# The attention's v loads are issued by ACT, at the end of each period

## The chip, the cores and the metric

The kernel runs on one core of a Trainium2 chip. A core has five engines, each with its own queue in program order: TensorE (PE; its weight loads are listed as PEld), VectorE (DVE), ScalarE (ACT), GpSimd (POOL) and SyncE (SP), which computes nothing and issues DMAs. Data moves between device memory and on-chip memory through 16 DMA engines. The metric is the device time of one execution in microseconds, given as the median of several runs; lower is better.

## What is computed

Two stages in 32-bit floats. First an attention in blocks of 64 positions, for 8 batches of 576 positions with 8 heads of 64:

```python
scores = scale * np.matmul(q_c, k_c.transpose(0, 1, 2, 4, 3))   # per block of 64
scores = scores - np.max(scores, axis=-1, keepdims=True)
attn = np.exp(scores)
attn = attn / (np.sum(attn, axis=-1, keepdims=True) + 1e-09)
out = np.matmul(attn, v_c)
```

Then a mixture of experts on the result x, with 4608 tokens of 512 and 8 experts of 512 x 1024 x 512. Each token goes to one expert:

```python
fresh_e = int(np.argmax(logits[b, s]))
if s == 0 or local_gate[b, s] < 0.5:
    e = fresh_e
else:
    e = prev_e if prev_e >= 0 else fresh_e
h = np.maximum(x[b, s] @ w1[e], 0.0)
out[b, s] = p[e] * (h @ w2[e])
```

## The kernel before

The attention works on 18 blocks of 256 tokens. For a block, `load_qk` (lines 115 to 130) brings q and k as `qt` and `kt`, `load_v` (132 to 141) brings v in four DMAs of 64 positions each. POOL regroups q and k by pairs of heads (`qr`, `kr`); PE transposes them (`tr`), ACT copies the results out (`qT`, `kT`, line 154). Then come the scores (`sc`, line 193), their row maxima and the subtraction on DVE (204, 207), the exponential on ACT (`pr`, 212), the transposes of `pr`, copied out by ACT (`pT`, 154), and the values: 32 matmuls for each half of the heads (`o`, line 242), which read v. DVE divides by the row sums and writes `xs` (lines 254 to 256). `xs` is transposed and copied out (`xT`), the router's logits are computed from it (`lg`, line 284), copied to `lT` (289), transposed back (293) and summed into `L` (299); line 302 stores `xs` with its logits to the device array `x_d`, from which the expert stage later gathers its tokens by index.

Buffers: v has two (`NV = 2`, line 112), used in turn; `qt` and `kt` three each; `xs` three; `pr` and `pT` two.

These steps are interleaved over blocks. The loop at line 754 plays 15 periods, i = 1 to 15; in each, the string `steady` says in which order the pieces are emitted:

```python
"steady": "lq s*8 s ra*2 h0 tp*8 va*4 s va h1 ra*2 tq*16 h2 va*4 va lv tx*8 s h3 pr*4 ",
```

Here `lq` loads q and k of block i+5, `s` are the scores of block i+1 (eight groups of matmuls, then the maxima, the subtraction, the exponential), `ra` the router of block i-3, `tp` the transposes of `pr` of block i, `va` the values of block i-1, `tq` the transposes of q and k of block i+2, `lv` the v load of block i+1, `tx` the transposes of `xs` of block i-2, `pr` the regrouping of block i+3, and `h0` to `h3` are places for pieces of the routing in late periods. After the played pieces, some periods append work on expert 0's weights: a load into `raw` (lines 764, 766), and in periods 4 to 11 a split of a piece of w1 into a high part, cast by ACT (`w1h`, line 96), and the rest, subtracted by DVE (`w1l`, line 97).

In the loop the order on PE, DVE, ACT and POOL is exactly the emitted one (`manual_schedule`); each engine runs its queue in that order and waits where a semaphore says so. SP's order is set by the planner. Before the loop, v of blocks 0 and 1 is loaded at line 479, outside of any order by hand; after it, the string `drain` orders the last blocks together with the first tiles of the expert stage, and `ld` in it is the v load of block 17. The expert stage then runs tiles of 128 tokens, with matmuls of lines 627 and 641.

All 72 v DMAs, like every other direct load and store, are issued by SP.

Of the kernel before, what the change touches and what calls it, by code (L numbers as in the profile page):

```python
# [56 lines left out]
    "t0": "VAVA",  # L57
    "t1": "AAAA",
    "t2": "AVAA",
    "steady": "lq s*8 s ra*2 h0 tp*8 va*4 s va h1 ra*2 tq*16 h2 va*4 va lv tx*8 s h3 pr*4 ",  # L60
    "hooks": [47, 47, 49, 49, 51, 52, 52, 52, 53, 53, 55, 56, 56, 57, 58, 60, 62, 62],
}

# [2 lines left out]
def tile_attention_then_moe(ctx: ExitStack, tc, q, k, v, wg, wl, w1, w2, out):  # L66
    nc = tc.nc
# [64 lines left out]
    def load_v(i):  # L132
        vt = vbuf[i % NV]
        for ch in range(4):
            t0 = 256 * i + 64 * ch
            b, s0 = t0 // S, t0 % S
            nc.sync.dma_start(
                vt[64 * (ch // 2):64 * (ch // 2) + 64, ch % 2, :, 0:D],
                v[b, :, s0:s0 + 64, :].rearrange("h s d -> s h d"),
            )  # L140
        return vt
# [164 lines left out]
    def ok(i):  # L306
        return 0 <= i < NS
# [125 lines left out]
    def a_pair(i, engs=(nc.gpsimd,) * 4):  # L433
        hd[i], fns = pair_heads(qk.pop(i), engs)
        return fns
# [13 lines left out]
    def a_tx(i, fine=False):  # L449
        xTs[i] = pa2.tile([P, 4, 256], F32, name="xT", bufs=1)  # L450
        return x_transposes(xss[i], xTs[i], fine)

    def a_ra(i, fine=False):
        return router(i, xTs.pop(i), xss.pop(i), fine)
# [19 lines left out]
    for i in range(3):  # L474
        qk[i] = load_qk(i, 2 if i == 0 else 1)
        if i == 0:
            nc.gpsimd.memset(wg9, 0.0)
        else:
            vts[i - 1] = load_v(i - 1)
    nc.sync.dma_start(wg9[:, :, 0:8], wg.rearrange("(c p) e -> p c e", p=P))  # L480
    nc.sync.dma_start(wg9[:, :, 8:9], wl.rearrange("(c p) e -> p c e", p=P))
    with tc.manual_schedule(engines=MAN):
        def load(store, fn, i):
            def go():
                store[i] = fn(i)
            return lambda: [go]
# [267 lines left out]
    for i in range(1, NS - 2):  # L754
        qs4 = dict(s=lambda: a_sa(i + 1), tp=lambda: a_tp(i), va=lambda: a_va(i - 1, True), tq=lambda: a_tq(i + 2))
        opt = dict(lq=load(qk, load_qk, i + 5) if ok(i + 5) else None,
                   lv=load(vts, load_v, i + 1) if ok(i + 1) else None,
                   pr=(lambda: a_pair(i + 3)) if ok(i + 3) else None, tx=(lambda: a_tx(i - 2)) if i >= 2 else None, ra=(lambda: a_ra(i - 3, True)) if i >= 3 else None)
        for h in range(4):
            opt[f"h{h}"] = (lambda h=h: [lambda: run(hooks[i, h])]) if (i, h) in hooks else None  # L760
        toks = [t for t in PAR["steady"].split() if opt.get(t.split("*")[0], 1) is not None]
        play(" ".join(toks), qs4 | {k: v for k, v in opt.items() if v is not None})
        if 1 <= i < 5:
            load_w1(0, i - 1)
        if i in (6, 8, 10, 12):
            load_w2(0, i // 2 - 3)
        if 4 <= i < 12:
            c, col = divmod(i - 4, 2)
            col = slice(512 * col, 512 * col + 512)
            split(w1h[c][:, col], w1l[c][:, col], raw1[c][:, col])  # L770
# [30 lines left out]
    def gather_full(t):  # L801
# [25 lines left out]
    ]  # L827
    queues = dict(
        s=lambda: sa, ld=load(vts, load_v, n), rt=lambda: sb, rk=sb_rank, of=lambda: offsets, oh=sb_onehots,
        sl=lambda: slots([pc, pc, pc], QB[1], QB[2], ((0, NT),), qs), ex=lambda: experts,  # L830
        g=lambda: [lambda t=t: gather_full(t) for t in (EARLY, EARLY + 1)],
# [148 lines left out]
```

## Time and profile before

| | us |
|---|---|
| median of three runs | 729.97 (729.54 to 731.80) |
| the profiled execution | 728.45 |
| its span, first to last instruction | 726.7 |
| PE busy over the span | 659.7 |
| ACT busy over the span | 270.7 |
| first and last start of a v load | 5.1 and 182.5 |

Times in the profile count from the start of the span. A row of the timeline gives the start, the duration, the engine, the line and the operation with what it writes and reads, a count where rows are merged, and in brackets how long the engine stood idle before it and what ended that. `SPq` is SP's queue: the duration of a DMA there is the time for which the issue held the queue, not the time of the transfer. In the windows view each engine has its busy time and its number of instructions, followed by PE's granted clock (1.00 is full speed), the mean busy share of the 16 DMA engines, and what they moved. DMA issues are not counted as busy time of an engine.

The page's list of DMA issues (operation, count, size of each, median time from issue to landing) has these of the attention:

```profile
x_d<-xs SPq DMA_DIRECT2D x18, 521.0 KB, 6.8
v<-in_v SPq DMA_DIRECT2D x72, 128.0 KB, 5.8
qt<-in_q SPq DMA_DIRECT2D x11, 512.0 KB, 6.5
kt<-in_k SPq DMA_DIRECT2D x11, 512.0 KB, 7.8
```

and the DMA queues (packets, megabytes, share of the 16 engines' span):

```profile
q1 hardware_dynamic: 96608, 75.70, 41.1%
q0 software_dynamic: 6160, 19.85, 8.3%
```

q1 is SP's queue, q0 that of POOL's indirect transfers.

### The profile page before, as it was taken

How to read it: one execution, taken by the hardware profiler on the slowest of the kernel's cores; microseconds unless marked ns; L12 is line 12 of the kernel's file. 1: busy time of each engine (PE TensorE's matmuls, PEld its weight loads, DVE VectorE, ACT ScalarE, POOL GpSimd, SP SyncE). 2: the span in 40 equal slices, each digit the busy share in tenths (PEclk: the TensorE clock that was granted, in tenths of full speed). 3: DMA queues.
4: the chain of work that ended last, by engine and by line, in shares of the span. 5: the costliest groups of instructions: out<-in, count | busy, mean ns of one | idle time of the engine just before them, and what ended most of it. 6: DMA issues, size and time to landing. Idle time of an engine off the chain costs nothing. (4 is left out here: it accounts for less than half of the span.)

```text
span 726.7 us, 17109 instructions
## 1 busy us (share of the span) xinstructions
PE 659.7 (91%) x5594; PEld 523.6 (72%) x5594; DVE 369.0 (51%) x860; ACT 270.7 (37%) x432; POOL 177.1 (24%) x222
## 2 busy tenths in 40 slices
PE   4786878878999999999999999999999999999981
PEld 4665666666677788777888887778877888777861
DVE  2564655788685585356232563472586323454310
ACT  3564655656422234441222443422454222432210
POOL 3321222234022233223121231331243212231100
PEclk9998999999999999999999999999999999999986
DMA  9999999968723144145111352441276211234100
GB/s 211 207 211 275 257 241 236 272 144 191 229 89 118 46 161 141 57 142 173 33 48 43 95 171 83 147 156 47 90 240 221 75 47 35 89 121 140 40 29 15
DMA packets 102928, 97.49 MB, mean 134 GB/s; under 512 B 42672, under 2 KB 79536, under 8 KB 102768
## 3 DMA queue, kind: packets, MB, share of 16 engines
q1 hardware_dynamic: 96608, 75.70, 41.1%
q0 software_dynamic: 6160, 19.85, 8.3%
q8 instruction: 78, 1.28, 0.8%
q14 instruction: 82, 0.67, 0.3%
HBM read 76.48 MB, written 19.56 MB: 132 GB/s over the span
## 5 line engine op out<-in xcount | busy, mean ns | idle before, releaser
L641 PE MATMUL y<-w2h,hp 128*128 128x512 f32 x608 | 204.7, 407 | 9.8 <-DVE hp L591 6.2
L627 PE MATMUL h<-w1h,xp 128*128 128x512 f32 x608 | 178.3, 403 | 0.0
L641 PEld LDWEIGHTS y<-w2h,hp 128*128 128x128 f32 x608 | 115.8, 191 | 38.9 <-DVE hp L591 8.9
L627 PEld LDWEIGHTS h<-w1h,xp 128*128 128x128 f32 x608 | 111.4, 189 | 23.9 <-ACTq L861 0.2
L641 PE MATMUL y<-w2l,hp 128*128 128x512 f32 x304 | 121.9, 401 | 0.0
L700 POOL DMA_INDIRECT out<-ysb,sidx x38 | 41.1, 1082 | 274.3 <-DVEq L861 197.0
L627 PE MATMUL h<-w1l,xp 128*128 128x512 f32 x304 | 95.9, 397 | 0.0
L590 ACT CAST hp<-tr 128x512 fp32r<-128x512 f32 x76 | 41.2, 589 | 107.7 <-PE tr L588 100.7
L591 DVE TENSOR_TENSOR xp<-tr,xp 128x512 fp32r<-128x512 f32 x39 | 27.0, 691 | 104.6 <-ACTq L861 66.9
L699 DVE TENSOR_SCALAR ysb<-y,ppr 128x512 f32<-128x512 f32 x35 | 26.2, 748 | 94.2 <-PE y L641 81.7
L627 PEld LDWEIGHTS h<-w1l,xp 128*128 128x128 f32 x304 | 57.0, 188 | 14.7 <-DVEq L861 0.7
L641 PEld LDWEIGHTS y<-w2l,hp 128*128 128x128 f32 x304 | 58.2, 191 | 12.4
L680 ACT ACTIVATE hsb<-h 128x1024 f32<-128x1024 f32 x35 | 36.0, 1027 | 67.0 <-PE h L627 64.3
L591 DVE TENSOR_TENSOR hp<-tr,hp 128x512 fp32r<-128x512 f32 x76 | 49.3, 686 | 13.8 <-ACT hp L590 12.1
L613 ACT ACTIVATE pex<-pex 128x8 f32<-128x8 f32 x38 | 7.9, 209 | 119.8 <-DVE pex L612 119.8
L97 DVE TENSOR_TENSOR w1l<-raw,w1h 128x1024 fp32r<-128x1024 f32 (+1 forms) x29 | 40.9, 1428 | 22.9 <-ACT w1h L96 22.7
L594 POOL DMA_INDIRECT xg<-x_d,gidx x36 | 36.6, 1017 | 41.0 <-issue 24.4
L156 POOL COPY qr<-qt 128x512 f32<-128x512 f32 x34 | 20.0, 617 | 101.1 <-issue 71.3
L242 PE MATMUL o<-v,pT 64*64 64x65 f32 x1152 | 29.0, 232 | 16.4 <-DVE xs L256 12.6
L588 PE MATMUL tr<-ident,hsb 128*128 128x128 f32 x304 | 40.2, 273 | 0.3 <-ACT hsb L680 0.3
L242 PEld LDWEIGHTS o<-v,pT 64*64 64x64 f32 x1152 | 22.6, 140 | 24.8 <-DVE xs L256 15.2
L97 DVE TENSOR_TENSOR w2l<-raw,w2h 128x1024 fp32r<-128x1024 f32 x21 | 39.9, 1953 | 0.9 <-issue 0.9
(173 smaller groups left out, 832.9 us busy)
## 6 DMA issues: line engine op xcount, KB each, us to landing
raw<-in_moe_w SPq DMA_DIRECT2D x72, 512.0 KB, 4.6
x_d<-xs SPq DMA_DIRECT2D x18, 521.0 KB, 6.8
v<-in_v SPq DMA_DIRECT2D x72, 128.0 KB, 5.8
qt<-in_q SPq DMA_DIRECT2D x11, 512.0 KB, 6.5
kt<-in_k SPq DMA_DIRECT2D x11, 512.0 KB, 7.8
qt<-in_q SPq DMA_DIRECT2D x6, 256.0 KB, 6.3
kt<-in_k SPq DMA_DIRECT2D x6, 256.0 KB, 6.2
qt<-in_q SPq DMA_DIRECT2D x4, 384.0 KB, 6.1
```

What stands on the lines that cost most here:

```text
L97: (lo_eng or nc.vector).tensor_tensor(lo, raw, hi.bitcast(F32), ALU.subtract)
L156: eng.tensor_copy(dst, src)
L242: nc.tensor.matmul(o[64 * cp:64 * cp + 64, cc, DV * h:DV * h + D + 1], pT[64 * cc:64 * cc + 64, 4 * j + h, 64 * cp:64 * cp + 64], vt[64 * ...
L588: nc.tensor.transpose(ps[:, n], src_of(n), ident)
L590: return [tr, lambda: nc.scalar.copy(hi, box["ps"]), lambda: V.tensor_tensor(lo, box["ps"], hi.bitcast(F32), ALU.subtract)]
L591: lambda: V.tensor_tensor(lo, box["ps"], hi.bitcast(F32), ALU.subtract)]
L594: nc.gpsimd.indirect_dma_start(out=dst, out_offset=None, in_=src, in_offset=bass.IndirectOffsetOnAxis(ap=gidx[t].bitcast(U32), axis=0))
L627: nc.tensor.matmul(hs[:, j], xs[a][:, c], W1[w][c][:, 512 * j:512 * j + 512], start=(c == 0 and n == 0), stop=(c == 3 and n == 2))
L641: nc.tensor.matmul(y, hx[f // 4][a][:, f % 4], W2[w][c][:, f % 2, :], start=(f == 0 and n == 0), stop=(f == 7 and n == 2))
L680: nc.scalar.activation(hsb, hs.rearrange("p j f -> p (j f)"), AF.Relu)
L699: either(mix, lambda: V.tensor_scalar(ysb, y, pr, None, ALU.mult), lambda: y_mixed(ysb, y, ym, pr))
L700: nc.gpsimd.indirect_dma_start(out=out, out_offset=bass.IndirectOffsetOnAxis(ap=sidx[t].bitcast(U32), axis=0), in_=ysb, in_offset=None, bo ...
```

## The change

The four DMAs of `load_v` are issued by ACT instead of SP, everywhere it is called: before the loop, in it and in the drain. In the loop the load's place in the emitted order moves from before the x transposes (`tx`) to behind them and behind the last `s`, which is the exponential. As ACT's order is the emitted one, its four issues stand there between the exponential and what the period appends.

```diff
-    "steady": "lq s*8 s ra*2 h0 tp*8 va*4 s va h1 ra*2 tq*16 h2 va*4 va lv tx*8 s h3 pr*4 ",
+    "steady": "lq s*8 s ra*2 h0 tp*8 va*4 s va h1 ra*2 tq*16 h2 va*4 va tx*8 s lv h3 pr*4 ",
...
         for ch in range(4):
             t0 = 256 * i + 64 * ch
             b, s0 = t0 // S, t0 % S
-            nc.sync.dma_start(
+            nc.scalar.dma_start(
                 vt[64 * (ch // 2):64 * (ch // 2) + 64, ch % 2, :, 0:D],
                 v[b, :, s0:s0 + 64, :].rearrange("h s d -> s h d"),
             )
```

The bytes, the buffers and the number of DMAs stay the same.

## The prediction

> **What bounds the kernel now.** Read first the page's head, then the busy time by stage (the windows view), because the change touches only the attention, which fills the first quarter of the span.
>
> ```profile
> span 726.7 us, 17109 instructions
> PE 659.7 (91%) x5594; PEld 523.6 (72%) x5594; DVE 369.0 (51%) x860; ACT 270.7 (37%) x432; POOL 177.1 (24%) x222
> ```
>
> ```profile
> core 0: us, PE busy (x) PEld busy (x) DVE busy (x) ACT busy (x) POOL busy (x), PEclk, DMA share, GB/s
> 60.00:70.00 10.00, 6.93 (x152) 5.84 (x152) 3.84 (x9) 3.47 (x6) 0.00 (x0) 0.66 1.13 267
> ...
> 160.00:170.00 10.00, 8.20 (x188) 6.45 (x188) 9.72 (x32) 5.36 (x9) 8.28 (x15) 1.00 0.49 107
> ...
> 0.70:146.00 145.30, 110.05 (x2272) 89.45 (x2272) 77.78 (x183) 78.09 (x133) 38.95 (x92) 0.94 1.13 241
> ...
> 113.24:124.97 11.73, 8.64 (x171) 6.90 (x170) 6.07 (x15) 6.11 (x11) 2.28 (x4) 0.89 1.06 252
> 124.97:133.39 8.42, 7.69 (x171) 6.29 (x170) 5.57 (x14) 5.62 (x10) 2.28 (x4) 0.95 1.20 246
> ```
>
> The last two rows are one period each of the steady loop, from one start of the scores to the next: 8.42 us when nothing stalls, 11.73 when something does. PE works about 8 us of each, so 8.42 is near its floor. Up to 146 us the DMA engines are full (a share of 1.13, since packets overlap). SP's own timeline shows what that does to the queue that issues all loads and stores (columns: start, duration, queue, line):
>
> ```profile
> 36.63 5.71 SPq L137 DMA_DIRECT2D v<-in_v  x4
> ...
> 45.25 4.92 SPq L137 DMA_DIRECT2D v<-in_v  x4
> ...
> 56.68 3.63 SPq L137 DMA_DIRECT2D v<-in_v  x4
> ...
> 103.75 0.57 SPq L302 DMA_DIRECT2D x_d<-xs  x1
> 104.42 4.24 SPq L137 DMA_DIRECT2D v<-in_v  x4
> 108.70 1.76 SPq L93 DMA_DIRECT2D raw<-in_moe_w  x1
> 110.55 1.32 SPq L125 DMA_DIRECT2D qt<-in_q  x1
> ...
> 152.18 2.92 SPq L137 DMA_DIRECT2D v<-in_v  x4
> ```
>
> Each begins within 0.1 us of the end of the one before: SP is held by the engines it feeds. At 152 us, with the DMA share near a half, the same four v loads still hold it 2.92 us. What does this cost the compute engines? The waits of DVE between 26.9 and 172.3 us, and one stall in the timeline:
>
> ```profile
> DVE xs L256 <- DMA x_d<-xs: 12.1, 6, 5.5
> ```
>
> ```profile
> 121.41 0.69 DVE L256 TENSOR_TENSOR xs<-o,rs 128x512 f32<-128x512 f32 x1 [2.14 <-DMA x_d<-xs]
> ```
>
> DVE may not overwrite an xs buffer until the store that read it has landed; that is the stall of the 11.73 period. PE pays twice for it (its own timeline):
>
> ```profile
> 111.59 0.70 PE L242 MATMUL o<-v,pT 64*64 64x65 f32 x32
> 112.22 1.09 PE L164 MATMUL tr<-ident,xs 128*128 128x128 f32 x8
> 113.24 1.16 PE L193 MATMUL sc<-kT,qT 64*64 64x64 f32 x64
> ...
> 122.16 0.99 PE L242 MATMUL o<-v,pT 64*64 64x65 f32 x32 [1.97 <-DVE xs L256]
> 123.08 1.97 PE L164 MATMUL tr<-ident,xs 128*128 128x128 f32 x8
> 124.97 1.52 PE L193 MATMUL sc<-kT,qT 64*64 64x64 f32 x64
> ...
> 161.15 0.70 PE L242 MATMUL o<-v,pT 64*64 64x65 f32 x32 [1.94 <-DVE xs L256]
> ```
>
> After 1.97 us of idleness the same three groups take 4.48 us in place of 2.95: 1.53 more at a lower granted clock (0.89 in that window, 0.66 in the worst). After 1.94 us at 161.15 the first group, 0.70 us, did not slow. So an idle stretch of about 2 us costs the slow clock in some cases, and I charge half of 1.53, 0.75.
>
> **The change part by part.** It removes four issues per period from SP, which has no compute behind it, and puts them on ACT, which has. The cost is worked out from ACT's order at a period's end, with DVE and PE beside it (timeline of all engines, the rows of a stall-free end; the issues will stand between the first and the second row):
>
> ```profile
> 93.76 1.07 ACT L212 ACTIVATE pr<-pr 128x1024 f32<-128x1024 f32 x1
> ...
> 94.71 0.62 ACT L96 CAST w1h<-raw 128x512 fp32r<-128x512 f32 x1
> ...
> 95.37 0.69 DVE L97 TENSOR_TENSOR w1l<-raw,w1h 128x512 fp32r<-128x512 f32 x1 [2.00 <-ACT w1h L96]
> 95.57 1.07 ACT L154 COPY pT<-tr 128x512 f32<-128x512 f32 x2 [0.24 <-PE tr L164]
> 95.90 0.70 PE L242 MATMUL o<-v,pT 64*64 64x65 f32 x32
> 95.98 1.28 DVE L204 TENSOR_REDUCE mx<-sc 128x8 f32<-128x512 f32 x2
> ...
> 97.18 0.41 DVE L289 COPY lT<-lg 128x256 f32<-128x256 f32 x1
> ...
> 97.65 0.44 PE L293 MATMUL lg<-ident,lT 128*128 128x128 f32 x2 [1.05 <-DVE lT L289]
> ```
>
> *How long ACT is held.* Call it L. The trace has no DMA issued by ACT; SP's durations for these very transfers are the nearest (all v issues, minimum, median and maximum):
>
> ```profile
> L137 SPq DMA_DIRECT2D v<-in_v x72: 595/765/2243, 5.1 to 182.5; - x72
> ```
>
> The bounds are 4 x 0.595 = 2.38 us and the 5.71 at 36.63; I take the median, 4 x 0.765 = 3.06 us. A wait for the buffer adds nothing: its last reader, the second group of values, runs ahead of the x transposes whose copies ACT has already made.
>
> *From when.* The cast starts 0.95 us after the exponential starts, 0.12 before that one's end, so ACT hands out work ahead of an end; how far, the trace does not show. I let the issues begin with the exponential's start. At the other end, after its end, each period costs 1.07 us more; the other way, one copy ahead, about 0.5 us less (an estimate: the two pT copies of the row at 95.57 take 1.07 together). The Trainium skill (PSUM — Partial Sum Buffer, Engine vs sequencer instructions) says the sequencer waits only for earlier instructions to be dispatched, which is the value I take; no run here shows it yet.
>
> *Periods with a weight split (eight, loop passes 4 to 11).* The cast slips from 0.95 after the exponential's start to L, 2.1 later. DVE stands in order behind it: w1l, the row maxima and the lT copy, and PE's logit transpose waits for lT already now. ACT's pT copy and PE's values slip as much. So PE loses 2.1, plus 0.75 for the clock, on a floor of 8.42: 11.3 us. The eight intervals behind these loads now run between two starts of the scores (PE's timeline):
>
> ```profile
> 34.15 1.16 PE L193 MATMUL sc<-kT,qT 64*64 64x64 f32 x64 [0.22 <-ACT kT L154]
> ...
> 66.04 1.93 PE L193 MATMUL sc<-kT,qT 64*64 64x64 f32 x64
> ...
> 143.41 1.16 PE L193 MATMUL sc<-kT,qT 64*64 64x64 f32 x64
> ```
>
> 143.41 - 66.04 = 77.4; eight times 11.3 is 90.4: **+13.0**. The removed store waits are in this already, as the floor is a stall-free period: with v gone from SP a store no longer queues behind the last period's v loads.
>
> *The three before (34.15 to 66.04, 31.9 us).* No split there; what slips is the pT copy, 1.81 after the exponential's start. The three v rows of that stretch, 5.71, 4.92 and 3.63, average 4.75; less 1.81 is 2.95. Three times (8.42 + 2.95 + 0.75) = 36.4: **+4.5**, although the long stall of 5.5 us goes.
>
> *The four after (from 143.41).* 2.92 - 1.81 = 1.1 each; DVE, busy 9.72 of 10 us at 160 to 170, sets the pace there, so I count half: **+2.2**, from 0 to 4.4.
>
> *Start and drain.* The first two loads are eight issues ahead of all else on ACT: 8 x 0.765 = 6.1 us against ACT's first work at
>
> ```profile
> 6.01 1.28 ACT L154 ACT_TABLE_LOAD   x1 [6.01 <-DMA qt<-in_q]
> ```
>
> and they share the engines with the first q and k. But SP reaches the third block of q and k earlier. **+1.5**, from -3 (q and k early) to +6. The drain's load holds ACT once while PE has other work: **+1**, from 0 to 2.9.
>
> Sum: 13.0 + 4.5 + 2.2 + 1.5 + 1 = +22.2. The profiled execution took 728.45; the median of the runs is 729.97, 1.5 higher. 728.45 + 22.2 + 1.5 = **752 us**. Nothing later is touched: the expert stage is released by the routing at the attention's end and shifts as a whole.
>
> **The rivals.**
>
> *Faster: the store waits go and ACT's hold is hidden.* Place: the boundary between periods. For it: DVE's 12.1 us of waits and the clock lost behind them stand in the trace, and ACT is busy only 5.6 of 8.42 us. With no hold at all the eight intervals give 77.4 - 67.4 = 10 and the three 31.9 - 25.3 = 6.6, so -16.6 is the bound; the full DMA engines keep about half of it: -9, **721 us**. It decides from L of about 2.5: there (no clock loss) the eight give +2.4, the three (8.42 + 0.7) x 3 = 27.4, -4.5, the rest some +2, in all nil. Four issues at the least duration seen, taken one copy ahead, pass that point. Against it: L has been that short only on an unloaded queue, and a period this short loads it.
>
> *No change: the transfers set the pace.* SP's queue is never empty until 146 us; if the engines' work alone makes a period 9.7 us, holds and stalls trade places: **730 us**, 728 to 732. The stall-free 8.42 periods speak against it.
> The Trainium skill (DMA: Bandwidth & Descriptors, Issuing engines are not separate DMA queues) says that all queues run on the same 16 engines and a second issuer saves only issue time; by it this change has no bandwidth to gain.
>
> *Much slower: the two queues hold each other up.* If an issue of ACT must wait while one of SP is being taken, L grows by SP's blocked issues. The weight row and the store row (1.76, 0.57) stand near the boundary, so about +2: L = 5.1, and the clock lost every time: 8 x (8.42 + 4.15 + 1.53) = 112.8, +35; the three 8.42 + 4.95 + 1.53 each, +13; with the rest some +54: **784 us**.
> The Trainium skill (Perfetto Trace Analysis, DMA Instruction — HWDGE (DVE, Sync)) describes one descriptor generator, locked by one sequencer at a time; that is this rival's rule, and with a single issuer before, the trace can neither bear it out nor refute it.
>
> **How the numbers follow.** Forecast, ACT's hold outweighs the stalls: 0.64 (735 to 768 by L from 2.7 to 3.6 and the start of the hold). Faster rival 0.18, no change 0.08, mutual hold 0.10. A measurement of this kernel can tell about 0.3% (2 us) from no change, so: faster 0.18, same 0.08, slower 0.74. The range drops about half of the fast rival and most of the slowest: 722 to 772.
>
> **What would show it.** Right: ACT's queue shows four v issues of 0.6 to 1 us behind each exponential; the cast and the pT copy start later after it by L; PE's values wait for ACT and its logit transpose for lT; DVE's waits for the x store vanish; stalled or not, the steady intervals are near 11 us; the windows there show a clock under 0.95 and a smaller DMA share. Wrong: ACT's issues under 0.5 us each, or intervals below 9.7; a clock of 1.00 would take 0.75 off each; if store waits remain, SP was not what delayed the stores; issues above 1.2 us speak for the mutual hold.

## The result, and the profile after

| | before | after |
|---|---|---|
| median, us | 730.62 (729.54 to 731.80) | 753.89 (750.96 to 754.24) |
| ratio, with its 95% interval | | 1.0326 (1.0298 to 1.0355) |
| span of the profiled execution | 726.7 | 749.2 |
| mean granted TensorE clock | 0.974 | 0.972 |

The change makes the kernel 3.3% slower. The forecast was 752. (The median of before is now of four runs, the 729.97 given ahead was of three.) First the head of the page of after, and its rows by stage (PE, PEld, DVE, ACT, POOL busy, then the clock, the DMA share and GB/s); the last three rows are the stretches that the prediction priced:

```profile
span 749.2 us, 17059 instructions
...
PE 659.5 (88%) x5594; PEld 524.9 (70%) x5594; DVE 369.6 (49%) x860; ACT 271.8 (36%) x432; POOL 177.6 (24%) x222
```

```profile
0.70:146.00 145.30, 97.79 (x1968) 81.56 (x1968) 62.83 (x144) 68.38 (x115) 34.55 (x84) 0.91 1.05 220
75.05:163.59 88.54, 64.79 (x1366) 52.60 (x1365) 49.45 (x122) 48.10 (x82) 18.53 (x32) 0.94 0.97 197
163.59:193.22 29.63, 23.69 (x534) 18.69 (x532) 23.46 (x79) 15.80 (x28) 11.66 (x20) 1.00 0.42 115
193.22:231.50 38.28, 33.13 (x424) 24.17 (x423) 23.25 (x64) 16.57 (x28) 3.09 (x3) 0.96 0.71 184
```

The same work on PE (659.5 us, against 659.7) is spread over a longer span. For comparison the same stretches of before:

```profile
66.04:143.41 77.37, 64.03 (x1366) 51.46 (x1365) 48.77 (x121) 47.08 (x81) 18.50 (x32) 0.94 1.15 252
143.41:172.28 28.87, 23.37 (x534) 18.69 (x532) 24.04 (x79) 15.88 (x28) 11.66 (x20) 1.00 0.64 152
172.28:204.90 32.62, 30.81 (x424) 22.46 (x423) 23.17 (x64) 16.58 (x28) 3.09 (x3) 1.00 0.81 232
```

In the eight intervals PE does the same 64 us of work at the same clock, 0.94, and 11.2 us later. The DMA engines now move 197 GB/s in place of 252: they are no longer what is short. What PE lacks is seen in one period of after (timeline of ACT, then rows of DVE and PE from the same stretch; `ACTq` is ACT's queue, where the issues stand):

```profile
98.08 0.60 ACTq L137 DMA_DIRECT2D v<-in_v  x1
98.18 0.59 ACT L154 COPY xT<-tr 128x512 f32<-128x512 f32 x1
98.66 1.07 ACT L212 ACTIVATE pr<-pr 128x1024 f32<-128x1024 f32 x1
98.73 2.02 ACTq L137 DMA_DIRECT2D v<-in_v  x3
...
100.79 0.62 ACT L96 CAST w1h<-raw 128x512 fp32r<-128x512 f32 x1 [1.06 <-issue]
```

```profile
101.44 0.69 DVE L97 TENSOR_TENSOR w1l<-raw,w1h 128x512 fp32r<-128x512 f32 x1 [3.23 <-ACT w1h L96]
102.05 1.28 DVE L204 TENSOR_REDUCE mx<-sc 128x8 f32<-128x512 f32 x2
103.25 0.41 DVE L289 COPY lT<-lg 128x256 f32<-128x256 f32 x1
...
103.72 0.44 PE L293 MATMUL lg<-ident,lT 128*128 128x128 f32 x2 [2.19 <-DVE lT L289]
```

This is the chain that the prediction wrote down: issue, cast, w1l, maxima, lT, PE. The first issue starts 0.58 us before the exponential, while the copies of xT still run; the cast starts 2.13 us after the exponential's start, where before it was 0.95. The other seven periods are alike: the eight casts start 2.13 to 3.77 us after their exponentials, 2.62 on average, and the logit transpose starts 2.93 us after the cast, as in most periods before. The waits between 27 and 195 us sum it up (us in total, times, longest):

```profile
DVE w1l L97 <- ACT w1h L96: 28.1, 8, 4.9
...
PE lg L293 <- DVE lT L289: 19.2, 8, 3.9
```

Before, these were 16.6 (8, 2.8) and 4.5 (6, 1.0). The 13.0 us in seven waits of DVE for the x store are gone. All eight splits now cost PE a wait.

But there is a second thing, which the prediction did not have. ACT's start, and the first load in the loop:

```profile
0.74 11.75 ACTq L137 DMA_DIRECT2D v<-in_v  x8
12.52 1.28 ACT L154 ACT_TABLE_LOAD   x1 [12.52 <-DMA v<-in_v]
...
41.82 8.52 ACTq L137 DMA_DIRECT2D v<-in_v  x4
...
50.39 1.07 ACT L154 COPY pT<-tr 128x512 f32<-128x512 f32 x2 [9.29 <-DMA v<-in_v]
```

Four issues hold ACT for 8.5 us. The answer for line 137 between 41 and 52 us (minimum, median and maximum of one in ns, first and last start) says that no issue is long:

```profile
L137 ACTq DMA_DIRECT2D v<-in_v x4: 602/602/603, 41.8 to 49.7; - x4
```

The four take 0.60 us each, 2.4 of the 8.52; the rest is waiting between them. What ACT waits for there is the subject of the last section on the experiments.

### The profile page after: what moved, and what is told of

The parts are those of the page before. It is cut to its first block, busy times and chain, and to the rows that moved or that the text cites. A ratio compares the mean times of both kernels' runs of the same rounds, so it can differ in the third digit from the quotient of the medians.

```text
span 749.2 us, 17059 instructions
## 1 busy us (share of the span) xinstructions
PE 659.5 (88%) x5594; PEld 524.9 (70%) x5594; DVE 369.6 (49%) x860; ACT 271.8 (36%) x432; POOL 177.6 (24%) x222
## 5 line engine op out<-in xcount | busy, mean ns | idle before, releaser
L641 PE MATMUL y<-w2h,hp 128*128 128x512 f32 x608 | 201.6, 401 | 10.0 <-DVE hp L591 6.1
L641 PEld LDWEIGHTS y<-w2h,hp 128*128 128x128 f32 x608 | 113.5, 188 | 38.3 <-DVE hp L591 8.3
L641 PE MATMUL y<-w2l,hp 128*128 128x512 f32 x304 | 120.0, 395 | 0.0
L700 POOL DMA_INDIRECT out<-ysb,sidx x38 | 41.2, 1084 | 270.4 <-DVEq L861 184.6
L590 ACT CAST hp<-tr 128x512 fp32r<-128x512 f32 x76 | 41.2, 589 | 107.5 <-PE tr L588 102.2
L591 DVE TENSOR_TENSOR hp<-tr,hp 128x512 fp32r<-128x512 f32 x76 | 49.3, 686 | 13.7 <-ACT hp L590 11.2
L164 PE MATMUL tr<-ident,qr 128*128 128x128 f32 x144 | 24.6, 325 | 23.6 <-ACT qr L154 14.6
L588 PE MATMUL tr<-ident,hsb 128*128 128x128 f32 x304 | 40.2, 273 | 0.3 <-ACT hsb L680 0.3
L588 PEld LDWEIGHTS tr<-ident,hsb 128*128 128x128 f32 x304 | 35.3, 140 | 6.7 <-ACT w2h L96 1.2
```

The source lines that it names most:

```text
L164: nc.tensor.transpose(box["ps"][:, n], src_of(n), ident)
L588: nc.tensor.transpose(ps[:, n], src_of(n), ident)
L590: return [tr, lambda: nc.scalar.copy(hi, box["ps"]), lambda: V.tensor_tensor(lo, box["ps"], hi.bitcast(F32), ALU.subtract)]
L591: lambda: V.tensor_tensor(lo, box["ps"], hi.bitcast(F32), ALU.subtract)]
L641: nc.tensor.matmul(y, hx[f // 4][a][:, f % 4], W2[w][c][:, f % 2, :], start=(f == 0 and n == 0), stop=(f == 7 and n == 2))
L700: nc.gpsimd.indirect_dma_start(out=out, out_offset=bass.IndirectOffsetOnAxis(ap=sidx[t].bitcast(U32), axis=0), in_=ysb, in_offset=None, bo ...
```

## The experiments

All ratios are against the kernel before, run on the same chip beside them. To see where each kernel gains or loses, this table gives, from the profiled execution of each, the six stretches that the prediction used, by the starts of the score groups on PE (line 193) and by the expert matmuls of line 641: "start" up to the score group that began at 34.15 before, then the three, the eight and the last three intervals, "drain" from the last score group to the first expert matmul of line 641, "experts" from there to the last one. Each row is one execution, while the ratio is from all runs; the four runs of one kernel can lie up to 10 us apart. The execution of "cast ahead of the issues" was the slowest of its four (743.66, median 740.0), that of "blocks 0 to 4 on SP, cast ahead, SP's order" the fastest (737.84, median 743.96).

| kernel | start | three | eight | last | drain | experts | ratio |
|---|---|---|---|---|---|---|---|
| before | 34.2 | 31.9 | 77.4 | 28.9 | 32.6 | 506.7 | |
| after | 40.2 | 34.8 | 88.5 | 29.6 | 38.3 | 502.6 | 1.0326 (1.0298 to 1.0355) |
| v on SP, new place | 32.8 | 33.0 | 76.5 | 28.9 | 32.8 | 505.0 | 1.0011 (0.9987 to 1.0034) |
| SP's order by hand alone | 32.6 | 34.5 | 76.4 | 29.4 | 35.5 | 505.0 | 0.9993 (0.9968 to 1.0019) |
| two of four on ACT | 36.2 | 31.9 | 82.1 | 28.9 | 32.4 | 504.2 | 1.0081 (1.0052 to 1.0110) |
| last five loads on ACT | 33.9 | 31.4 | 76.5 | 28.6 | 41.2 | 507.8 | 1.0084 (1.0061 to 1.0107) |
| blocks 0, 1 on SP | 33.9 | 38.8 | 91.7 | 29.6 | 34.1 | 505.0 | 1.0288 (1.0243 to 1.0332) |
| blocks 0 to 4 on SP | 32.4 | 32.6 | 99.3 | 29.6 | 38.3 | 505.3 | 1.0381 (1.0329 to 1.0434) |
| after, SP's order by hand | 40.6 | 29.8 | 92.6 | 30.1 | 34.3 | 503.8 | 1.0273 (1.0216 to 1.0330) |
| cast ahead of the issues | 40.2 | 37.7 | 79.9 | 29.6 | 33.8 | 505.5 | 1.0156 (1.0112 to 1.0200) |
| blocks 0 to 4 on SP, cast ahead, SP's order | 32.2 | 33.1 | 82.4 | 29.6 | 38.3 | 505.0 | 1.0214 (1.0154 to 1.0273) |
| blocks 0, 1 on SP, cast ahead, SP's order | 33.0 | 37.1 | 79.5 | 29.6 | 34.2 | 505.6 | 1.0135 (1.0080 to 1.0190) |
| load early in the period | 34.4 | 38.6 | 79.1 | 29.5 | 35.3 | 506.5 | 1.0190 (1.0133 to 1.0247) |
| issued by POOL | 32.7 | 37.4 | 88.1 | 29.3 | 37.1 | 505.3 | 1.0177 (1.0118 to 1.0235) |

### Place or issuer

The new place alone: the change with v issued by SP.

```diff
-            nc.scalar.dma_start(
+            nc.sync.dma_start(
```

> The change's new place in the order, but issued by SP as before. Theory (the engine that issues is what matters, not the place): the same as before within 3 us, 728 to 733. Rival (the later place makes v late or pushes the x stores back): 736 or more, with waits of PE's values for v.

Measured 1.0011. The place costs nothing; the store waits stay (16.6 us in 11 waits), since SP still issues everything. So the loss comes with the issuer. (ACT as issuer at the old place was not run.)

Half of it:

```diff
-            nc.scalar.dma_start(
+            (nc.scalar if ch % 2 else nc.sync).dma_start(
```

> Two of the four DMAs of every v load on ACT, two on SP. Theory (the cost is ACT's hold): the issues end about 0.7 us after the exponential starts, so neither cast nor pT copy slips by more than 0.3 us; the x stores still have less ahead of them on SP than before; the start loses about half of 6 us: 727 to 735. Rival (two queues hinder each other whatever the number): the issues on ACT take over 1.2 us each and the time stays above 745.

Measured 1.0081. On before's 730.62 this is 736.5 us, just over the 727 to 735 of the theory and well under the rival's 745; the median issue on ACT is 0.60 us, so the rival's sign is absent too. With two issues in place of four, the eight intervals lose 4.7 us in place of 11.2, and PE's waits for lT fall from 19.2 to 6.4 us.

### The cast behind the issues

ACT's cast of the weights is emitted ahead of the four issues, as a piece of its own (`wc`); the rest is the change.

```diff
-... va*4 va tx*8 s lv h3 pr*4 ",
+... va*4 va tx*8 s wc lv h3 pr*4 ",
...
+    def w1_cast(i):
+        c, col = w1_piece(i)
+        nc.scalar.copy(w1h[c][:, col], raw1[c][:, col])
```

> The change, with ACT's cast of the w1 piece emitted ahead of the four v issues in the eight periods that have one (DVE's subtraction stays at the period's end). Theory (what is on the path is the cast behind the issues, as DVE stands in order behind it and PE's logit transpose waits for lT): the waits of PE for lT fall from 19.2 us to about the 4.5 of before, the pT copy slips by under 1 us, the eight intervals shrink by 8 to 12 us: about 743. Rival (the pT copy is what PE waits for, or the transfers pace the period): the waits only move to the values, the eight intervals shrink by under 3 us: 751 to 754.

Measured 1.0156: half of the loss is gone, some 10 us (a median of 740.0; the ratio of after, times the 726.3 of before on that chip, is 750). It comes from where it should: the eight intervals are 79.9 in place of 88.5, and PE's waits for lT are back at 4.5 us in five waits (the row of the eight intervals, then PE's waits between 27 and 195 us):

```profile
77.92:157.79 79.87, 64.69 (x1365) 51.45 (x1364) 49.62 (x122) 47.51 (x82) 18.43 (x32) 0.94 1.10 217
```

```profile
PE lg L293 <- DVE lT L289: 4.5, 5, 1.0
```

In the table the kernels divide by this: with four issues of ACT ahead of the cast the eight take 88.5 to 99.3 us, with the cast ahead 79.1 to 82.4 (in the kernel that loads early the issues stand behind the copies of pT instead, far from the cast), with SP as issuer 76.4 to 77.4; POOL's kernel, 88.1, loses there in another way, told below. This step of the prediction is shown: 8.6 of the 11.2 us that the eight intervals lose come from the cast standing behind the issues.

### The start, and what it hides

The loads of blocks 0 and 1 go back to SP:

```diff
-            vts[i - 1] = load_v(i - 1)
+            vts[i - 1] = load_v(i - 1, nc.sync)
```

> The change, with the two v loads ahead of the loop issued by SP again; those in the loop and in the drain stay on ACT. Theory (ACT is held by its own issues): the first start of the scores, 14.23 us before and 19.86 after, comes back to about 14.5, and the 5 to 6 us lost there are won back: about 748. Rival (the start is paced by the transfers whichever queue issues them): what is won at the first scores is lost again by the sixteenth block, and the time stays at 752 to 754.

Measured 1.0288: nearly nothing, as the rival had it. The start is 6.3 us earlier, then ACT is held for 5.64 and 10.73 us in the next loads, and the last score group starts at 193.91, against 193.22 in after. SP's timeline in after had also shown that the planner, whose SP queue had no v loads left, drew all eight early weight loads forward to between 17 and 53 us. So the next kernel is after with SP's order written out by hand as emitted:

```diff
-    man = tc.manual_schedule(engines=MAN | {ET.Pool})
+    man = tc.manual_schedule(engines=MAN | {ET.Pool, ET.SP})
```

> The change, with SP's order in the loop emitted by hand as well: SP issues in the order of before, less the v loads (in the change the planner drew all eight weight loads ahead, to 16.9 to 53 us). Theory (the 8.5 us for which ACT was held by its first load in the loop come from the weight loads drawn ahead): that hold falls under 4 us, the interval behind it from 15.6 to about 10 us, and the time by 3 to 6 us, to about 1.026 times before. Rival (the engines are full there whatever the order): the hold stays above 6 us and the time at 1.032.

Measured 1.0273, between the theory's 1.026 and the rival's 1.032, and its interval holds both. The theory's sign is there: the first load in the loop holds ACT for 2.71 us in place of 8.52, and the three intervals take 29.8 us. But the eight lose it again (92.6). The control, the same edit in the kernel before:

> The kernel before, with SP's order in the loop written out as emitted and nothing else changed; v stays on SP. It is the control for the three kernels that had both. If the order by hand costs nothing: ratio 0.997 to 1.003, and the losses of those kernels (1.0135 to 1.019) belong to the second queue. Rival, the order by hand is itself their loss: 1.008 or more, with new waits for q and k or for a store in the loop.

Measured 0.9993: the order by hand alone costs nothing, so the losses of the kernels that have it are not its own.

### Versions that should have repaired it

If the start, the weights drawn forward and the cast were all, taking the three away should leave nothing:

```diff
-    "steady": "... tx*8 s lv h3 pr*4 ",
+    "steady": "... tx*8 s wc lv h3 pr*4 ",
...
-            vts[i - 1] = load_v(i - 1)
+            vts[i - 1] = load_v(i - 1, nc.sync)
...
-    man = tc.manual_schedule(engines=MAN | {ET.Pool})
+    man = tc.manual_schedule(engines=MAN | {ET.Pool, ET.SP})
```

> Three costs taken out together: v of blocks 0 and 1 issued by SP, the cast ahead of the v issues, SP's order of before; ACT issues the other v loads where the change has them. Theory (these three are the whole loss): within 3 us of before, ratio 0.998 to 1.006, with the first scores at 14, DVE's waits for the x stores gone and PE's waits for lT near 4.5 us. Rival (ACT's hold also costs by the pT copy, or the two queues hold each other): ratio 1.010 or more, with issues on ACT of over 1 us.

Measured 1.0135, a miss: the eight are good (79.5), but the three take 37.1 and ACT is held twice for over 7 us (rows below). The rival's ratio came, but not its sign: the median issue on ACT is 0.64 us. The two other ways were to issue v far from the exponential, and to take another engine with nothing to do there:

```diff
-    "steady": "... tp*8 va*4 s va ... tx*8 s lv h3 pr*4 ",
+    "steady": "... tp*8 lv va*4 s va ... tx*8 s h3 pr*4 ",
...
-                   lv=load(vts, load_v, i + 1) if ok(i + 1) else None,
+                   lv=load(vts, load_v, i) if i >= 2 else None,
...
```

The load of block 16 becomes a piece of the drain; what SP issues is as in the last kernel.

> v of blocks 0 and 1 by SP, SP's order by hand, and each later v load on ACT right behind the pT copies, where ACT then waits 1 to 2 us for the next transposes; it loads the block of the next period. Theory (the place on ACT decides, and ACT's hold can be hidden there): ratio 0.985 to 1.000, without waits for x stores and with no wait of PE's values for v. Rival (v then lands too late, or the qT copies slip by what the cast slipped before): 1.005 or more.

Measured 1.0190, a miss: the copies of qT slip in place of those of pT (PE waits 23.5 us for them).

```diff
-            nc.scalar.dma_start(
+            (eng or nc.gpsimd).dma_start(
```

> v of blocks 0 and 1 by SP, SP's order by hand, and each later v load issued by POOL at the end of the period behind its regrouping copies; ACT issues nothing. Theory (SP without v frees the x stores, and what cost time was ACT): the waits for x stores go and nothing holds ACT, ratio 0.980 to 0.998. Rival (the transfers set the pace, or POOL's issues of about 1 us each delay its regrouping): 1.00 or more, PE's transposes waiting for POOL.

Measured 1.0177, a miss. The ratio is the rival's, but PE's transposes do not wait for POOL, whose issues take 0.68 us (median); PE waits 7.5 us for v, and DVE still 6.7 us for x stores. With ACT free of any issue the kernel is still 1.8% slower. From the DMA issues between 27 and 75 us, first with POOL's queue beside SP's, then in the kernel before (count, KB of each, median us to landing):

```profile
qt<-in_q SPq DMA_DIRECT2D x5, 512.0 KB, 11.9
kt<-in_k SPq DMA_DIRECT2D x5, 512.0 KB, 12.9
```

```profile
qt<-in_q SPq DMA_DIRECT2D x5, 512.0 KB, 6.5
kt<-in_k SPq DMA_DIRECT2D x5, 512.0 KB, 7.9
```

With the DMA engines full, q and k land 5 us later once POOL's queue is beside SP's; with SP's order by hand and all v on SP they land in 7.2 and 8.1 us, so it is not the order. About the same bytes move between 27 and 75 us (11.1 MB, before 11.5), but in 13887 packets in place of 21761, so the transfers are not the same in all. PE also stops for 18.1 us with no wait named (5.8 before), on which see the last section. So this kernel shows a price of the second queue that is neither ACT's nor the cast's; how it divides between the later landings and PE's stops is not shown.

### Taking the full stretch out

ACT issues none of the loads while the DMA engines are fullest: v of blocks 0 to 4 from SP, once as the change, once with the cast ahead and SP's order by hand.

```diff
-            nc.scalar.dma_start(
+            (nc.sync if i < 5 else nc.scalar).dma_start(
```

> The change, but v of blocks 0 to 4 issued by SP, so that ACT issues none before the first weight split. Theory of parts: the start (+6.1 us) and the early stretch (+2.9) go, the eight intervals keep their +11 and the last stretch its +1: ratio 1.014 to 1.019. Rival, losses move rather than go: 1.024 or more, with the eight intervals above 90 us.

> As the one before, with ACT's cast of the weights emitted ahead of the four issues, and SP's order by hand. If what is left of the loss after the cast sits where the DMA engines are full (up to about 75 us): ratio 0.999 to 1.006, eight intervals 77 to 80 us, three about 32 us. Rival, any second queue costs PE in all periods: 1.010 or more.

Measured 1.0381 and 1.0214, both misses, to the rival's side. Start and three are as good as before's (32.4 and 32.6), and in the first kernel the eight are worse, 99.3. It is one interval that does it, from 76.99 to 97.42; the other seven average (99.3 - 20.4) / 7 = 11.3 us, the prediction's number. In the second kernel, too, one interval of 16.7 us makes the loss; the other seven average (82.4 - 16.7) / 7 = 9.4 us, no more than the 9.7 of before, so a second queue does not cost PE in all periods. In the long interval (ACT and DVE of the first of the two kernels):

```profile
80.13 7.81 ACTq L137 DMA_DIRECT2D v<-in_v  x3
...
87.98 0.62 ACT L96 CAST w1h<-raw 128x512 fp32r<-128x512 f32 x1 [9.23 <-DMA v<-in_v]
...
88.63 0.69 DVE L97 TENSOR_TENSOR w1l<-raw,w1h 128x512 fp32r<-128x512 f32 x1 [11.72 <-ACT w1h L96]
```

The last one goes to the other end: only the five loads of blocks 13 to 17.

```diff
-            nc.scalar.dma_start(
+            (nc.sync if i < 13 else nc.scalar).dma_start(
```

> The change for the last five v loads alone (blocks 13 to 17), where no weights are split and the DMA share is below a half; the others stay on SP, at the new place. The prediction had +2.2 us for the four intervals there and +1 for the drain (ratio about 1.004); the trace of after shows +0.8 for the four. Theory: hidden behind DVE, ratio 0.998 to 1.003, ACT's issues about 0.6 us each. Rival: 1.004 or more, with PE waiting on ACT's pT copies.

Measured 1.0084. The intervals are as expected: 28.6 us with v on ACT, 28.9 with it on SP; ACT's four issues stand beside DVE's long chain and cost nothing. The loss is nearly all in the drain, 41.2 against 32.8 us (32.6 before), and not where the rival placed it: PE has no wait for ACT's pT copies in these intervals. PE's pauses in the drain are shown in the last section.

### What ACT waits for between its issues

The long holds move about from kernel to kernel, and always come with a bracket on ACT's next instruction that makes no sense for it. After (a later period), blocks 0 and 1 on SP, and the first repaired version:

```profile
112.13 0.62 ACT L96 CAST w1h<-raw 128x512 fp32r<-128x512 f32 x1 [2.71 <-DMA x_d<-xs]
```

```profile
55.87 10.73 ACTq L137 DMA_DIRECT2D v<-in_v  x3
66.64 1.07 ACT L154 COPY pT<-tr 128x512 f32<-128x512 f32 x2 [11.98 <-DMA qt<-in_q]
```

```profile
40.95 7.63 ACTq L137 DMA_DIRECT2D v<-in_v  x3
...
56.35 7.21 ACTq L137 DMA_DIRECT2D v<-in_v  x3
63.60 1.07 ACT L154 COPY pT<-tr 128x512 f32<-128x512 f32 x2 [7.70 <-DMA x_d<-xs]
```

A copy from `tr` to `pT` needs neither q nor the stored x. It was the issue ahead of it that waited for them. The built program of after says why; this is ACT's list for the first load of the loop, with the semaphores that each instruction waits for:

```
30 L137 DMA v_119<-in_v 64x8x64 [waits DMAHW6_49,PE_49]
31 L137 DMA v_119<-in_v 64x8x64 [waits DMAHW3_49,DMAHW0_49,PE_49]
32 L137 DMA v_119<-in_v 64x8x64 [waits DMAHW2_49]
33 L137 DMA v_119<-in_v 64x8x64 [waits DMAHW4_49,PE_49]
34 L154 COPY pT<-tr 128x512 [waits PE_49] x2
```

The program has eight completion semaphores, DMAHW0 to DMAHW7, for all DMAs that SP and ACT issue. They are given out in turn, and before one is given out again, the issuing engine waits until the DMA that had it last has landed. As long as SP issued everything, these waits held nothing: in the attention of the kernel before, each of SP's issues that has one starts 0.19 us or more after the landing that it asks for. Now they hold ACT, and most of the DMAs that it waits for are SP's. The trace has the times of the landings; for the hold of 8.52 us in after, with SP's issues from its timeline:

```profile
33.41 1.57 SPq L125 DMA_DIRECT2D qt<-in_q  x2
35.03 1.31 SPq L90 DMA_DIRECT2D raw<-in_moe_w  x1
36.44 2.58 SPq L125 DMA_DIRECT2D kt<-in_k  x2
...
39.73 0.44 SPq L93 DMA_DIRECT2D raw<-in_moe_w  x1
...
42.26 2.67 SPq L125 DMA_DIRECT2D kt<-in_k  x1
```

| ACT's issue starts | the DMA whose semaphore it takes over | its last part landed |
|---|---|---|
| 41.82 | q (first of the two from 33.41) | 41.75 |
| 44.41 | weights, from 35.03 | 44.35 |
| 46.95 | k (second of the two from 36.44) | 46.93 |
| 49.74 | weights, from 39.73 | 49.67 |

Each of the four issues starts 0.02 to 0.07 us behind a landing. Counted over all issues of v, those that start within 0.15 us of the last landing on a semaphore they wait for, and later than their queue was free, are some 16 of 72 in after, about 18 us of waiting: about 6.3 of it at the start, 7.6 in this hold and just ahead of it. At the start most of that time is for ACT's own first loads, later nearly all of it is for SP's DMAs. By the same count ten of SP's issues are held in after as well, nearly 14 us. In the other kernels where ACT issues v early in the attention there are 5 to 20 of v, some 8 to 24 us; in the long interval of the kernel with blocks 0 to 4 on SP there are three, of 2.3, 2.7 and 3.2 us, for k, weights and q of SP; with all v on SP there are none, and none with the last five loads alone on ACT. For POOL the program uses other semaphores, and the count there is none, so what POOL's kernel loses is not this.

So with two issuers the eight semaphores come round while the transfers that had them are still under way. That would explain why the holds moved and did not go when the start, the weights or the first loads were put back. It is read from the program and from the landings in these traces (a few landings are missing from them, so the counts are approximate). A kernel in which ACT's loads have semaphores of their own was not tried, so what these waits cost in all is not shown.

## Why the prediction was right, point by point

The forecast of 752 us held, with 753.89 measured. The likeliest case, "ACT's hold outweighs the stalls", is what happened. By its own terms, after less before in the profiled executions:

| term | forecast | measured |
|---|---|---|
| start | +1.5 | +6.1 |
| three intervals | +4.5 | +2.9 |
| eight intervals | +13.0 | +11.2 |
| last intervals | +2.2 | +0.8 |
| drain | +1 | +5.7, then -4.1 in the experts |
| sum | +22.2 | +22.5 (spans) |

The sum is better than its parts: what is missed at the start and in the drain (+4.6 and +4.7) is offset by the three, the eight and the last intervals (-4.8 together) and by the experts (-4.1), which the forecast left untouched. That the total came so close is luck. The direction is not, and neither is the largest term.

- *How long ACT is held.* One issue was taken as 0.765 us, SP's median. On ACT the median is 0.646 and the least 0.602, so four hold it for 2.7 us (98.08 to 100.75 in the period shown), inside the bounds.
- *From when.* The issues start even earlier than at the exponential's start. The cast slips by 2.13 - 0.95 = 1.2 us in a good period, and by 2.62 - 0.95 = 1.7 on average, not by 2.1.
- *Eight intervals.* Their mean is 88.54 / 8 = 11.1, forecast 11.3. The chain named was the right one, and the kernel with the cast ahead shows it. Against the stall-free period (8.42 us, PE busy 7.69), PE is busy 64.79 / 8 = 8.10 us of each, so 0.4 for slower matmuls, forecast 0.75; and it is idle 2.2 us more, forecast 2.1. Of this idleness 1.7 is the slip of the cast; the rest, some 0.6, the forecast had no term for. The slower matmuls stand in three of the eight periods, at a clock of 0.85 to 0.87; in the other five it is 1.00. Of two in a row:

```profile
86.46:97.97 11.51, 8.82 (x171) 7.45 (x171) 5.74 (x15) 6.06 (x11) 2.29 (x4) 0.85 0.93 183
97.97:107.67 9.70, 7.51 (x171) 6.03 (x170) 5.87 (x15) 5.83 (x11) 2.29 (x4) 1.00 0.89 183
```

- *The fast rival.* It was to win below a hold of about 2.5 us. In the period shown the cast starts after 2.13 us, and on average after 2.62, so its condition was nearly met, and the kernel is still 3.3% slower. With 2.62 its working gives the eight intervals 8 x (8.42 + 1.67) = 80.7 us; they took 88.5. What that working leaves out is the slower matmuls and the other idleness, 1.0 us per period together, and the start.
- *Store waits.* Gone, as forecast. With SP as issuer at the new place they are even 3.6 us longer, and that kernel is no slower (1.0011), so a longer wait of DVE there is not simply added to the time. What winning them back is worth, no run shows by itself.
- *"A wait for the buffer adds nothing."* This is the step that failed. The buffer indeed adds nothing, but each issue carries a second wait, for the landing of an earlier DMA on its semaphore. It holds ACT for about 6.3 of 11.75 us at the start, which makes the miss there (8 x 0.60 and those 6.3 are 11.1, forecast 6.1), and for 6 us in the first load of the loop.
- *Three intervals.* They were forecast from SP's holds (4.75 each). What came is one interval of 15.6 us (40.22 to 55.84), then 11.4 and 7.8: the sum was near, the picture was not.
- *Four later.* Half of 1.1 each was too much; the kernel with the last loads alone shows nothing there, since DVE sets the pace.
- *The rival in which two queues hold each other up* did not come by its mechanism. Five of the 72 issues in after are over 1.2 us, the longest 1.45, and SP's k issue of 42.26 starts while ACT's of 41.82 (0.60 us) still stands. Its outcome, an ACT held by SP's transfers, is what the early holds look like, by the shared semaphores instead.
The Trainium skill (Perfetto Trace Analysis, DMA Instruction — HWDGE (DVE, Sync)) has one descriptor generator that one sequencer locks at a time; ACT's median of 0.646 against a least of 0.602 us leaves little room for that here.
- *The rival in which the transfers set the pace* is right about the room that there was: the share of the DMA engines up to 75 us is 1.10 before and 1.15 after. But it gives no loss, and after reaches the score group of 66.04 only at 75.05.
The Trainium skill (DMA: Bandwidth & Descriptors, Issuing engines are not separate DMA queues) says that a second issuer saves issue time alone. In this trace, too, the eight intervals gain no rate: 252 GB/s before and 197 after.

## What to carry to other kernels

A DMA issue is not free for the engine that carries it: count 0.6 us each on ACT's queue, look what stands behind it in that engine's order, and look in the program for what the issue itself waits for, above all the completion semaphores that it shares with other queues. A bracket that names a DMA which the instruction cannot need is the sign of such a wait, taken by an issue just ahead of it. Where an engine that only issues has room, its long holds cost less here than the same issues did on an engine with compute behind it; none of the versions tried here beats the kernel before.

## What was not expected of the hardware

ACT begins an issue while two instructions that it handed out earlier still have to run: in the rows above the first issue starts at 98.08, the second copy of xT at 98.18 and the exponential at 98.66. In the kernel with the cast ahead it is three: an issue starts at 95.08, the copy at 95.17, the exponential at 95.65 and the cast at 96.61.

PE stops inside a group of equal matmuls, with no wait named. The last score group of the attention takes one run of 64 (1.16 us) in the kernel before; with the last five loads on ACT, its timeline has:

```profile
170.45 1.08 PE L193 MATMUL sc<-kT,qT 64*64 64x64 f32 x49
172.22 0.34 PE L193 MATMUL sc<-kT,qT 64*64 64x64 f32 x4 [0.68 <-issue]
172.98 0.35 PE L193 MATMUL sc<-kT,qT 64*64 64x64 f32 x5 [0.42 <-issue]
173.73 0.35 PE L193 MATMUL sc<-kT,qT 64*64 64x64 f32 x4 [0.40 <-issue]
174.47 0.24 PE L193 MATMUL sc<-kT,qT 64*64 64x64 f32 x1 [0.39 <-issue]
175.19 0.36 PE L193 MATMUL sc<-kT,qT 64*64 64x64 f32 x1 [0.48 <-issue]
```

```profile
170.45:211.60 41.15, 35.98 (x424) 26.03 (x423) 23.14 (x64) 16.61 (x28) 3.08 (x3) 0.88 0.61 171
```

The group takes 5.1 us, and the drain then runs at a clock of 0.88, where the same stretch before had 1.00. The same pattern stands in after (194.79 to 197.91), in both kernels with blocks 0 to 4 on SP, and in SP's order by hand alone, where no ACT issue is near (the drain there is 35.5). So ACT's issues are not needed for it. Whether PE's instructions come late there is not shown: the trace has an instruction packet from 171.71 to 172.65 us in these pauses, but also one from 171.91 to 173.38 in the kernel before, which does not pause. The cause stays open, and with it the drain's 8.4 us in the kernel with the last loads on ACT, and the expert stage's 4.1 us less in after.
